# DeltaNet and gated FFN on one core: inverting the first two pairs' blocks in their own layout, and another order of work

## The chip, the cores and the metric

The kernel runs on one core of a Trainium2 chip. The metric is the device time of one execution in microseconds (us), lower is better. The engines are TensorE (PE; its weight loads are listed as PEld), VectorE (DVE), ScalarE (ACT), GpSimd (POOL) and SyncE (SP). SP only issues DMAs; ACT issues some too, and POOL a few at the start.

## The reference, cut to what matters

```python
B, H, S, D = 4, 8, 768, 48
def attn(q, k, v, beta):
    k_n = k / (norm(k, axis=-1) + 1e-6)
    state = zeros((B, H, D, D))
    for t in range(S):
        y[:, :, t] = einsum('bhd,bhde->bhe', q[:, :, t], state)
        v_old = einsum('bhde,bhd->bhe', state, k_n[:, :, t])
        state += beta[:, :, t] * outer(k_n[:, :, t], v[:, :, t] - v_old)
x = y.transpose(0, 2, 1, 3).reshape(B * S, H * D)      # 3072 x 384
h = x @ w_in                                           # w_in 384 x 2048
out = (h * cos(h)) @ w_out                             # w_out 2048 x 384
```

All of it is float32. The inputs w_in and w_out arrive in a 64-bit format, which the kernel takes apart into words.

## The kernel before

**Units and pairs.** The sequence is cut into 24 units of 32 tokens (`NU`, `C`). Within a unit the recurrence becomes a triangular system for each of the 32 (batch, head) blocks. For unit n the kernel turns keys and queries (`turn`), multiplies them with the keys (`gram`, tile p_g), scales the key part into a triangular block g (`gram_keys`) and masks the query part into tt (`gram_queries`). Then it applies the state to keys and queries (`through_state`, p_kq), subtracts (`right_side`), solves with the inverse of the block (`solve`, p_u), updates the state (`update`, p_s), adds the in-chunk part (`within`, p_kq) and turns the result into x (`features`, p_z). Each unit's state needs the unit before it. Two units are a pair m; a pair's 256 tokens are one step p of the feed-forward part.

**Inversion.** Pair m's blocks go to DRAM (`gram_put`, g_dr) and come back with one block on each partition (`gram_get`, gb). `invert` eliminates column by column: a product (line 675, tile part), then a subtraction (line 682, tile z), on POOL. The result goes to DRAM again (`put`, z_dr) and comes back in the layout of the solve (`get`, zt). Pair 0 (`HALVED` = 1) differs: `fold` lays the two 16-wide diagonal blocks of each 32-wide block over each other, the elimination has 15 columns and runs on DVE, and units 0 and 1 are solved in halves: `solve_half` (p_w), `between` with the off-diagonal block (p_v), then `solve` (p_u) from halves_z.

**Feed-forward.** Steps 0 and 1 compute h plainly (`hidden`, p_h, one product for two of the eight groups of 256 columns), later steps with 20 products of sums of x and of w_in (`x_sum` line 968, `in_sums`, `layer` line 1053). Step 0 multiplies with w_out plainly (`output`, line 1076), later ones with seven products (`product` line 1133) of sums of gate blocks (`left_sum`, line 1149) and of w_out (`right_sum`).

**Weights.** 12 tiles of w_in and 16 of w_out are loaded (`narrow_load`, tile pairs of a pool of eight shared with the gates and others), split by ACT (`narrow_split`), shifted by DVE (`narrow_shift`), added by POOL (`narrow_add`).

**Order.** Every step is a task with an engine, dependencies and the buffers it makes and frees. `Order.LINE` is a list of numbers: all tasks in the sequence in which they are written out. Each engine and each DMA queue runs its own in that sequence, and an instruction that waits holds up all behind it on its engine. `Order.OTHER` lists the tasks that go to the other queue (ACT instead of SP) or the other engine (POOL or DVE). Costs and due times in `add` are a planner's; at run time they do nothing.

Of the kernel before, what the change touches and what calls it, by code (L numbers as in the profile page):

```python
# [46 lines left out]
class Order:  # L47

    OTHER = {
        ('gram_put', 0), ('gram_get', 0), ('put', 0), ('q', 3), ('gram_get', 1), ('k', 4),  # L50
        ('gram_get', 2), ('k', 7), ('weights', 3), ('weights', 5), ('weights', 6), ('weights', 9),
        ('weights', 10), ('weights', 14), ('weights', 15), ('weights', 17)
# [3 lines left out]
0 1971 1 2 10 11 12 7 3 37 4 72 14 38 39 42 15 73 1972 13 1975 43 96 1973 97 40 1974 16 44 17 1976  # L56
18 1979 19 45 20 79 46 75 99 76 48 100 77 80 47 1983 78 1980 104 1977 49 81 50 1981 1978 105 1987
82 1982 1984 51 9 101 131 1985 84 52 1991 132 1988 53 36 102 1986 1995 54 155 106 1992 8 55 56 107
108 109 1989 22 1996 1999 1993 1990 134 74 1997 1994 135 1998 110 21 41 111 23 83 2000 138 2003 57
2001 136 139 24 2002 137 2007 156 25 112 26 98 27 28 2004 186 113 29 2011 2008 2005 30 187 32 31  # L60
114 210 2009 140 103 2015 33 58 141 211 142 115 189 143 2012 190 34 2019 59 35 2013 133 2016 60
2006 2017 61 2020 2023 679 116 2021 2018 62 680 684 2027 63 117 681 241 682 2024 683 64 685 2025
2031 689 2022 65 2028 2026 2029 157 118 66 5 6 68 67 2035 69 818 159 265 2032 686 86 687 2033 160
688 2030 690 2039 691 161 2034 2036 119 2010 719 692 2037 2014 162 163 164 693 191 2040 2043 70
822 694 87 71 243 85 165 244 2038 193 695 2041 2047 699 245 194 696 819 697 158 166 88 2042 700
731 704 89 167 2051 2048 698 120 192 2044 90 701 92 168 91 702 709 2045 2055 2052 296 703 93 705
2053 94 714 169 95 706 710 2049 2056 711 707 121 2059 712 708 195 715 2046 747 196 197 198 2050
716 717 170 2063 2060 720 718 122 748 713 749 123 735 2067 2064 2061 752 2054 124 2062 736 171 125
2057 753 2071 127 750 823 320 757 2065 128 126 754 2066 129 751 145 130 2058 755 2075 758 172 214
146 2072 739 762 298 2073 215 299 2068 756 216 248 173 821 721 763 217 2076 2069 2079 764 219 188  # L70
732 767 765 759 766 760 825 2070 772 174 768 2077 247 2080 769 2078 761 770 2074 2081 220 777 771
2082 221 144 740 773 826 300 782 774 269 218 775 778 222 722 829 268 779 776 743 147 723 744 223
780 733 724 725 783 820 212 249 827 302 726 830 224 148 835 303 149 737 213 151 727 152 150 225
175 784 824 351 781 153 176 154 788 785 728 177 226 828 745 270 178 729 179 787 227 831 790 730
789 834 180 793 746 182 375 181 794 183 246 228 184 786 796 185 791 832 250 798 200 792 242 251
799 252 836 253 840 800 741 353 842 839 843 271 801 229 844 851 272 845 738 274 855 841 852 301
846 802 856 273 847 354 324 848 804 803 849 857 734 355 797 859 275 201 853 806 860 199 833 807
854 850 837 742 858 808 266 304 276 866 809 277 323 795 861 867 202 862 870 203 810 278 863 267
864 204 206 357 871 868 207 205 279 874 869 230 231 865 875 356 878 406 805 872 838 811 280 873
232 876 812 879 233 877 898 880 234 813 894 358 882 899 281 235 883 895 237 236 896 430 886 900  # L80
881 208 897 884 209 901 238 814 282 885 325 902 815 887 379 239 816 888 240 903 906 890 953 889
305 904 955 378 907 956 922 306 960 908 905 957 892 307 308 910 958 891 255 954 408 909 959 893
326 297 283 911 925 918 817 919 964 928 912 327 968 923 965 329 929 920 924 969 966 921 972 256
961 967 409 914 962 970 963 284 328 931 971 915 410 330 973 913 979 916 930 981 980 917 974 933
926 983 975 285 927 934 331 984 982 935 332 254 411 985 936 976 987 321 986 937 988 333 359 977
991 412 978 257 992 989 258 1011 939 334 413 990 259 940 261 941 260 993 461 262 1007 932 942 335
994 322 286 943 1008 287 995 944 352 938 336 288 996 945 1009 289 1012 997 290 1013 998 292 376
337 1014 946 291 1015 485 1001 947 1016 263 949 1010 293 264 380 338 999 294 1000 950 295 1002
1017 434 360 1019 951 1005 361 362 1003 1018 948 1020 381 1066 1006 310 1068 1021 1004 1069 339
1031 1035 382 1070 463 384 1071 1032 1077 1067 1022 1081 1072 1078 311 363 1073 1038 1036 1082  # L90
1074 464 1027 1079 1041 309 414 1033 465 1083 1080 383 1042 1037 952 1084 1034 385 1085 386 1076
1028 1087 340 1023 1075 1044 1029 1024 1086 433 312 1094 313 387 1092 1043 468 314 1095 1093 1046
316 1030 1096 317 315 388 1025 467 1098 1088 1097 341 1099 1026 1100 342 435 1047 389 1101 1039
1104 488 1040 1102 1045 343 1103 1048 1105 489 390 1120 1089 1108 344 1090 1106 1049 516 1091 345
347 1109 346 1050 1124 391 1125 1052 1107 1126 318 1054 1112 319 1121 1110 1127 1122 392 1055 1128
540 1123 348 1056 466 1111 349 1057 1114 350 1113 1058 1129 1179 1132 1051 1186 1130 1059 1181
1115 1182 1053 1116 1180 1060 1131 415 1183 1061 1149 365 1184 518 1189 1133 1118 1187 416 1134
417 1185 1062 418 1119 393 1117 436 519 1140 1190 437 1141 1194 439 377 1063 1195 1142 1198 1191
1143 1196 1188 1199 1064 520 1192 1144 1135 394 1148 1193 440 366 438 1197 407 1151 1145 1150 1207
1154 1146 1205 1208 1136 1155 1147 364 1137 1157 1138 1211 441 1159 431 1139 1200 442 1152 1160  # L100
1201 1156 395 1206 1153 367 1209 368 443 1065 1161 1212 1210 369 1162 1158 371 571 370 1213 372
444 1202 1163 469 1203 373 1165 374 1204 1214 396 1167 523 445 1217 490 1215 1218 522 1168 1216
1237 397 1233 1169 1166 446 462 1238 1221 1164 1239 1219 1234 1222 398 1220 1235 1225 399 1223 447
1226 400 1170 1224 1240 402 595 432 1227 1245 403 1171 1236 448 401 1241 1172 1228 1229 1173 1242
544 404 1231 1246 405 1243 1175 1230 1247 1232 1176 573 1248 1292 1293 470 1177 1253 1302 449 420
1244 486 1294 1254 1303 1295 1257 471 1296 1307 1262 1304 1297 473 472 1255 1261 1298 1258 1299
1256 491 1300 1259 1178 419 1264 1301 1308 492 574 1249 1311 421 1174 575 1250 494 1305 1312 487
1267 1309 1306 1320 543 524 1310 1268 1251 1260 1318 493 495 496 1321 1270 1319 1263 578 1252 1313
1265 1322 1314 1324 450 1323 422 1272 1315 497 1273 1266 577 1316 423 1274 1326 1275 498 1325 424
1269 426 626 521 1328 427 1327 425 1276 499 1329 428 1317 451 429 1346 1278 452 1330 1280 500 545  # L110
453 1334 1331 598 454 1281 1350 1335 1271 1282 1347 517 501 1332 1348 1283 1336 1333 599 455 1351
1337 1349 457 1352 1284 1279 458 650 502 1354 1353 1338 456 1340 1277 459 1341 1342 460 1339 1285
1405 1355 541 1407 525 1356 1286 1406 576 1344 1358 1408 1287 526 1409 1288 1359 1410 528 1345 503
1289 1360 527 1361 546 1290 475 1370 1343 628 1416 547 1357 1420 549 629 1366 1374 1411 548 1421
1371 1415 1417 1377 1367 1412 504 1372 1291 630 1418 1375 1380 1376 1422 1419 550 1373 1381 1423
579 1368 1413 1424 1362 1414 1431 1369 474 1425 1363 1426 1432 542 1433 1427 632 1435 551 476 1364
1383 1436 552 1434 505 1439 1428 1437 1365 1440 633 1429 477 1385 553 1438 1443 478 1441 1378 479
1379 481 1442 554 1386 482 1384 1459 1444 1447 1430 1387 480 1448 1463 1460 1445 555 1464 1449
1446 506 1465 1388 1450 1389 507 1461 1466 572 1391 631 556 1467 1462 508 1393 1453 1468 1394 1454
1469 509 1395 557 1470 510 1382 512 511 1457 483 1458 1451 484 600 513 1455 514 1452 530 654 515  # L120
1456 1471 1396 1518 580 1390 1520 1397 1472 596 1521 581 1522 1473 1398 582 1523 1392 1479 583
1525 1529 1399 1519 1474 1533 1530 1524 1480 1400 601 558 1481 1401 602 603 1475 604 1482 1534
1402 634 1531 1403 1535 1532 1476 1483 1487 1526 1536 1484 1528 1490 1477 1404 1527 559 1485 605
1478 1537 1493 1488 1539 1538 1486 1494 1540 1489 1546 1541 1496 1547 1542 560 531 606 1544 1543
# [65 lines left out]
def kernel(  # L190
# [1060 lines left out]
    def unit(n):  # L1251
# [71 lines left out]
        if second:  # L1323
            inverse(m)
# [369 lines left out]
```

## Time and profile before

| | us |
|---|---|
| median of 3 runs | 659.93 |
| lowest, highest | 659.56, 664.02 |
| span of the profiled execution | 657.8 |
| PE busy | 598.3 |
| DVE, ACT, POOL busy | 485.7, 259.7, 448.2 |
| start of the first product of step 0's h | 71.3 |
| end of the last matmul | 652.95 |

The profile is of one execution; its times start at the span's begin. A line of a timeline gives the start, the length, the engine, the line of the kernel, the operation, its tiles (out<-in), shape and count, and in brackets the idle time before it and what ended that. A matmul of float32 leaves two records. Engine rows give busy time; DMA issues and waits are not in it. The chain of waits is followed back from the last instruction, at each step to what released it.

### The profile page before, as it was taken

The numbers are of one execution on the slowest core, as the hardware profiler recorded it, in microseconds if no ns is written. First come the engines' busy times: TensorE is split into PE (matmuls) and PEld (weight loads), VectorE is DVE, ScalarE is ACT, GpSimd is POOL, SyncE is SP. The second block draws the span as 40 slices with busy tenths as digits, with TensorE's granted clock in tenths as the row PEclk, the third lists the DMA queues.
The fourth block names the chain that finished last, engine by engine and source line by source line (L and its number), as shares of the span: only waits on it lengthen the run. The fifth ranks groups of instructions, "written<-read, shape, count | busy, mean of one in ns | idle before, by whom it ended". The sixth has DMA issues, their size and how long they took to land.

```text
span 657.8 us, 27560 instructions
## 1 busy us (share of the span) xinstructions
PE 598.3 (91%) x11960; PEld 561.2 (85%) x11960; DVE 485.7 (74%) x886; ACT 259.7 (39%) x446; POOL 448.2 (68%) x844
## 2 busy tenths in 40 slices
PE   3316889989989999999999999899999999999997
PEld 3305869877889999999999999899999999999996
DVE  6685487878878887877779868778768687566772
ACT  3432456452223542435434523542523534335340
POOL 4458698878888888868968848868688589203000
PEclk9999799989999999999999999999999999999999
DMA  8876674465254453452243454432412400200000
GB/s 171 198 159 150 164 182 124 121 124 75 55 101 70 62 103 61 75 98 45 51 95 53 84 91 67 80 53 37 95 29 43 88 5 15 45 3 26 0 25 25
DMA packets 215644, 51.78 MB, mean 79 GB/s; under 512 B 207076, under 2 KB 210420, under 8 KB 215524
## 3 DMA queue, kind: packets, MB, share of 16 engines
q1 hardware_dynamic: 204516, 43.39, 34.8%
q10 hardware_dynamic: 10752, 6.20, 3.7%
q8 instruction: 94, 1.54, 1.0%
q0 software_dynamic: 256, 0.44, 0.3%
q14 instruction: 26, 0.21, 0.1%
HBM read 39.24 MB, written 10.75 MB: 76 GB/s over the span
## 4 chain that ended last, share of the span: by engine, by line
PE 52%; POOL 23%; DMA 10%; SPq 5%; issue 5%; DVE 4%; ACT 1%; ACTq 0%; POOLq 0%; DVEq 0%
PE p_out L1133 19%; PE p_h L1053 19%; POOL part L675 10%; POOL z L682 10%; PE p_h L875 3%; DMA qp<-in_q_dram 3%; PE p_kq L732 2%; DMA gb<-g_dr 2%; PE p_u L795 2%; PE p_s L818 2%; PE p_kq L835 2%; PE p_o L1133 2%; DMA g_dr<-g 1%; DMA pairs<-in_moe_w_in_dram 1%; POOL x_sum L968 1%
## 5 line engine op out<-in xcount | busy, mean ns | idle before, releaser
L675 POOL TENSOR_TENSOR part<-z,gb 128x126 f32<-128x126 f32 (+22 forms) x341 | 154.0, 452 | 57.2 <-DMA gb<-g_dr 15.4
L682 POOL TENSOR_TENSOR z<-z,part 128x126 f32<-128x126 f32 (+22 forms) x341 | 155.4, 456 | 26.7
L1133 PE MATMUL p_out<-w_out,g_ffn 128*128 128x192 f32 x672 | 121.2, 328 | 0.4 <-ACT o L1172 0.4
L1133 PEld LDWEIGHTS p_out<-w_out,g_ffn 128*128 128x128 f32 x672 | 107.8, 190 | 1.7 <-ACT o L1172 0.6
L1133 PE MATMUL p_out<-w_sum,g_ffn 128*128 128x192 f32 x496 | 89.1, 329 | 0.3 <-issue 0.3
L932 ACT ACTIVATE turns<-turns,halfpi 128x512 f32<-128x512 f32 x96 | 68.3, 720 | 47.0 <-DVE turns L923 46.8
L1053 PE MATMUL p_h<-x_sum,w_in 128*128 128x128 f32 x640 | 83.2, 278 | 1.7 <-POOL x_sum L968 1.7
L1133 PEld LDWEIGHTS p_out<-w_sum,g_ffn 128*128 128x128 f32 x496 | 79.7, 190 | 1.2 <-issue 0.4
L1053 PEld LDWEIGHTS p_h<-x_sum,w_in 128*128 128x128 f32 x640 | 77.3, 192 | 3.5 <-POOL x_sum L968 2.1
L1149 DVE TENSOR_TENSOR g_ffn<-g_ffn 128x512 f32<-128x512 f32 x88 | 64.5, 737 | 12.6 <-PE p_out L1133 11.7
L916 ACT ACTIVATE turns<-g_ffn,quarter_turn 128x512 int32<-128x512 f32 x70 | 50.4, 720 | 55.9 <-DVE g_ffn L1070 37.2
L1070 DVE TENSOR_TENSOR g_ffn<-g_ffn,p_h 128x512 f32<-128x512 f32 x80 | 54.0, 682 | 15.8 <-PE p_h L1053 13.1
L935 DVE TENSOR_TENSOR g_ffn<-turns,g_ffn 128x512 f32<-128x512 f32 x70 | 52.9, 758 | 11.3 <-ACT turns L932 11.3
L923 DVE SCALAR_TENSOR_TENSOR turns<-g_ffn,turns 128x512 f32<-128x512 f32 x70 | 52.8, 760 | 8.4 <-ACT turns L916 8.2
L1053 PE MATMUL p_h<-x_sum,in_sum 128*128 128x128 f32 x400 | 53.4, 278 | 2.0 <-POOL x_sum L968 1.5
L875 PE MATMUL p_h<-x_ffn,w_in 128*128 128x128 f32 x384 | 49.5, 289 | 2.9 <-DVE g_ffn L935 2.3
L1053 PEld LDWEIGHTS p_h<-x_sum,in_sum 128*128 128x128 f32 x400 | 49.4, 192 | 3.0 <-POOL x_sum L968 1.7
L875 PEld LDWEIGHTS p_h<-x_ffn,w_in 128*128 128x128 f32 x384 | 47.3, 203 | 4.2 <-issue 2.4
L1185 DVE SCALAR_TENSOR_TENSOR o<-p_out,o 128x192 f32<-128x192 f32 x74 | 25.2, 353 | 31.8 <-PE p_out L1133 30.8
L486 POOL TENSOR_TENSOR knrm<-ksum,halves 128x16 f32<-128x16 f32 (+1 forms) x14 | 38.5, 2752 | 11.1 <-DVE ksum L474 10.9
L1053 PE MATMUL p_h<-x_ffn,w_in 128*128 128x128 f32 x320 | 42.5, 277 | 0.0
L1053 PEld LDWEIGHTS p_h<-x_ffn,w_in 128*128 128x128 f32 x320 | 39.2, 192 | 0.4
(122 smaller groups left out, 933.2 us busy)
## 6 DMA issues: line engine op xcount, KB each, us to landing
pairs<-in_moe_w_out_dram SPq DMA_DIRECT2D x13, 384.0 KB
vp<-in_v_dram SPq DMA_DIRECT2D x96, 48.0 KB
gb<-g_dr SPq DMA_DIRECT2D x18, 256.0 KB
out_dram<-o SPq DMA_DIRECT2D x23, 192.0 KB
pairs<-in_moe_w_in_dram SPq DMA_DIRECT2D x7, 512.0 KB
kp<-in_k_dram SPq DMA_DIRECT2D x128, 24.0 KB
z_dr<-z SPq DMA_DIRECT2D x11, 256.0 KB
zt<-z_dr SPq DMA_DIRECT2D x88, 32.0 KB
```

The source lines that it names most:

```text
L486: nc.gpsimd.tensor_tensor(out=scales[m][2][:, part], in0=sums[m, part.start][:, 0:n], in1=halves[:, 0:n], op=ALU.pow,)
L675: eng.tensor_tensor(out=part, in0=z[:, 0:rows, j, None].to_broadcast(shape), in1=a[:, j, None, j + 1 :].to_broadcast(shape), op=ALU.mult,)
L682: eng.tensor_tensor(out=behind, in0=behind, in1=part, op=ALU.subtract)
L875: nc.tensor.matmul(p_h[:, i], w_in[:, t, (4 * k + i) * 128 : (4 * k + i + 1) * 128], xts[p][:, t, unit * 128 : (unit + 1) * 128], start=(i ...
L916: nc.scalar.activation(turns[p, f], hidden_of(p, f), AF.Identity, bias=quarter_turn, scale=TURN)
L923: nc.vector.scalar_tensor_tensor(out=r, in0=hidden_of(p, f), scalar=TURN, in1=t, op0=ALU.mult, op1=ALU.subtract,)
L932: nc.scalar.activation(r, r, AF.Sin, bias=halfpi, scale=2.0 * math.pi)
L935: nc.vector.tensor_tensor(out=place(p, f), in0=step_of(rests.pop((p, f)), f), in1=step_of(hidden_of(p, f), f), op=ALU.mult,)
L1053: nc.tensor.matmul(p_h[:, e], in_block(*w)[:, e], x_of(p, b), start=new and e == 0, stop=True, skip_group_check=True,)
L1070: nc.vector.tensor_tensor(out=part_of(p, to), in0=part_of(p, one), in1=part_of(p, two), op=op)
L1133: nc.tensor.matmul(p_o, left(p, part, a)[:, e % 4], right(e, b), start=(e == 0), stop=(e == FT // 2 - 1), skip_group_check=True,)
L1149: either(("left", p, x, s), nc.vector, nc.gpsimd).tensor_tensor(out=left(p, s, to), in0=left(p, s, one), in1=left(p, s, two), op=op)
```

## The change

- Pairs 0 and 1 (`ROWED` = 2) are both inverted as 16-blocks, in the layout in which their products come: rows of a block on partitions. Matmuls with 0/1 matrices (`picks`, made on DVE in memory that w_sum uses later) copy row j of each 16-block to all 16 of its partitions in PSUM (`rows`, p_r). Units 0 and 1 are eliminated on DVE, each by itself (groups 0 and 1); units 2 and 3 together on POOL (group 2), for which ACT copies the rows from PSUM (`rows_copy`).
- The DRAM passages of pairs 0 and 1 and pair 1's inversion of 31 columns are gone. Units 2 and 3 are now solved in halves too. ACT takes part in `fold` and `unfold`.
- Weights are staged in six slots in in_sum and w_sum; a load waits for the addition of the tile six places before it.
- The table load of ACT's sine comes first on ACT; the far part of the constants is loaded later, by SP; beta is spread in two parts; `scale` and `weigh` are split into smaller tasks.
- The dependency of each plain hidden product on the one before it is gone, and a hidden step's g tile is made at the gate.
- `LINE` and `OTHER` are new: 36 load, store and transfer tasks go to ACT's queue instead of 7, 61 sums of x go to DVE, 37 sums of gates to POOL, and a few sums of weights change engine.

```diff
-    HALVED, HC = 1, C // 2
+    ROWED, HC = 2, C // 2
...
+    halfpi = const.tile([128, 1], FP, name="halfpi")
+    nc.gpsimd.memset(halfpi, math.pi / 2.0)
+    warm = const.tile([128, 1], FP, name="warm")
+    nc.scalar.activation(warm, halfpi, AF.Sin)
+
     load(0, "k")
     load(0, "q", nc.scalar)
...
+    picks = w_sum[:, 0 : FT // 4].rearrange("p e a c -> p (e a c)")[
+        :, 0 : (HC - 1) * 128
+    ].rearrange("p (j m) -> p j m", m=128)
+
+    def make_picks(js):
+        by_row = ident.rearrange("p (g r) -> p r g", r=HC)
+        nc.vector.tensor_copy(
+            picks[:, js].rearrange("p j (g r) -> p j g r", r=HC),
+            by_row[:, js, :, None].to_broadcast([128, js.stop - js.start, 128 // HC, HC]),
+        )
...
+    stages = [
+        in_sum[:, 2 * i : 2 * i + 2].rearrange("p a e c -> p (a e c)") for i in range(4)
+    ] + [
+        w_sum[:, FT // 4 :].rearrange("p e a c -> p (e a c)")[:, i : i + 4 * TOK]
+        for i in (0, 4 * TOK)
+    ]
...
-        pairs = ffn_pool.tile([128, 4, TOK], U32, name="pairs", tag="g", bufs=GATES)
-        words[t] = pairs.rearrange("p a t -> p (a t)")[:, 0 : 2 * n]
+        words[t] = stages[t % len(stages)].bitcast(U32)[:, 0 : 2 * n]
...
+    GROUPS = [(0,), (1,), (2, 3)]
+    ON_POOL = (2,)
...
+    def rows(r, s):
+        f, x = of_group(r)[0], of_group(r)[3]
+        p_r = p_rows[r, s] = bank("h", [128, 4 * H * HC], "p_r").rearrange(
+            "p (j x i) -> p j x i", x=x, i=HC
+        )
+        js = rows_at(r, s)
+        for k, j in enumerate(js):
+            i = 1 + (js[0] if r in ON_POOL else j)
+            nc.tensor.matmul(
+                p_r[:, k, :, i:], picks[:, j], f[:, :, i:],
+                start=True, stop=True, skip_group_check=True,
+            )
...
+    def eliminate(r, s):
+        f, z, scratch, x = of_group(r)
+        eng = nc.gpsimd if r in ON_POOL else nc.vector
+        p_r = p_rows.pop((r, s))
+        for k, j in enumerate(rows_at(r, s)):
+            part = scratch[:, :, j + 1 :]
+            eng.tensor_tensor(
+                out=part,
+                in0=z[:, :, j, None].to_broadcast([128, x, HC - 1 - j]),
+                in1=p_r[:, k, :, j + 1 :],
+                op=ALU.mult,
+            )
+            behind = z[:, :, j + 1 :]
+            eng.tensor_tensor(out=behind, in0=behind, in1=part, op=ALU.subtract)
+
+    def unfold(n):
+        zts[n] = half_zt[n]
+        z = row_tile(n)[:, 0, n % 2, :, HC:]
+        for a in range(2):
+            to = zts[n][:, :, HC * a : HC * a + HC]
+            if ("unfold", n) in Order.OTHER:
+                nc.scalar.activation(to, z, AF.Copy, scale=in_half[:, a : a + 1])
+            else:
+                nc.vector.tensor_scalar(to, z, in_half[:, a : a + 1], None, op0=ALU.mult)
...
-        if n < 2 * HALVED:
+        if n < 2 * ROWED:
             add(("solve_half", n), "PE", few, lambda: solve_half(n), ready,
...
         add(("weights", t), "SP", 0.45, lambda: narrow_load(t),
-            [("weights", t - 1)] if t else [],
-            makes=[("g", ("pairs", t))], moves=1.8 * c, due=LOADS + 2 * t)
+            ([("weights", t - 1)] if t else [])
+            + ([("add", t - len(stages))] if t >= len(stages) else []), moves=1.8 * c, due=LOADS + 2 * t)
```

## The prediction

> **What bounds the kernel now.** I read the page's engine shares, then busy time by stage, then PE's timeline at the start, the chain of waits, and the rows that price the new work.
>
> ```profile
> span 657.8 us, 27560 instructions
> ...
> PE 598.3 (91%) x11960; PEld 561.2 (85%) x11960; DVE 485.7 (74%) x886; ACT 259.7 (39%) x446; POOL 448.2 (68%) x844
> ```
>
> By stage: its ends and length (us), busy us of PE, PEld, DVE, ACT and POOL with their counts, then clock, DMA share, GB/s.
>
> ```profile
> 0.00:71.30 71.30, 27.68 (x844) 23.03 (x844) 46.66 (x125) 25.50 (x46) 43.01 (x64) 0.95 0.72 166
> 71.30:101.00 29.70, 26.62 (x568) 23.94 (x567) 20.53 (x34) 16.98 (x32) 23.75 (x33) 0.94 0.77 189
> 101.00:154.50 53.50, 51.07 (x1004) 45.68 (x1004) 42.18 (x75) 26.90 (x49) 44.44 (x85) 0.97 0.51 109
> 154.50:470.90 316.40, 310.94 (x6693) 292.21 (x6693) 251.78 (x440) 122.22 (x207) 258.59 (x506) 1.00 0.42 71
> ```
>
> PE idles 71.3 - 27.7 = 43.6 us before 71.3 and only 59.5 - 43.6 = 16 afterwards. Its work is the bound once it has work, so a gain must come from the start. PE's timeline there:
>
> ```profile
> 49.84 1.81 PE L762 MATMUL p_w<-vp,halves_z 32*32 32x48 f32 x64 [1.16 <-ACT kq_t L544]
> ...
> 69.47 1.90 PE L762 MATMUL p_w<-rhs,halves_z 32*32 32x48 f32 x64 [2.20 <-ACT x_ffn L862]
> 71.29 4.50 PE L875 MATMUL p_h<-x_ffn,w_in 128*128 128x128 f32 x24
> 75.73 0.88 PE L762 MATMUL p_v<-u_half,halves_z 32*32 32x48 f32 x64
> 76.54 2.94 PE L875 MATMUL p_h<-x_ffn,w_in 128*128 128x128 f32 x24
> ...
> 101.16 1.10 PE L795 MATMUL p_u<-rhs,zt 32*32 32x48 f32 x60 [0.34 <-DMA zt<-z_dr]
> ```
>
> Unit 0's first solve (p_w) waits until 49.8 because pair 0's blocks go through DRAM before and after the inversion; unit 2's (p_u, 101.2) because pair 1's inversion holds POOL from 50.3 to 89.4. The passages, in the chain of waits:
>
> ```profile
> 19.19 5.80 DMA g_dr<-g
> 25.55 3.25 DMA gb<-g_dr
> ...
> 50.40 5.16 DMA halves_z<-z_dr
> ...
> 90.51 4.01 DMA z_dr<-z
> ...
> 96.13 4.98 DMA zt<-z_dr
> ```
>
> One elimination step (a product, then a subtraction) on DVE and on POOL, from their timelines:
>
> ```profile
> 33.16 0.23 DVE L675 TENSOR_TENSOR part_v<-p_i,gb 128x64 f32<-128x64 f32 x1
> 33.42 0.23 DVE L682 TENSOR_TENSOR p_i<-p_i,part_v 128x64 f32<-128x64 f32 x1
> ```
>
> ```profile
> 63.10 0.43 POOL L675 TENSOR_TENSOR part<-z,gb 128x136 f32<-128x136 f32 x1
> 63.61 1.22 POOL L682 TENSOR_TENSOR z<-z,part 128x136 f32<-128x136 f32 x1
> ```
>
> **PE's ledger.** I price every matmul of both orders by late, undisturbed rows: 8 records of p_h 0.89, 8 of p_out 1.30 (2.69 when 384 wide), a state product 1.30, a Gram, p_w, p_v, p_u or in-chunk product 0.81, p_s 0.82, p_z 0.33, a turn 1.04. Before: 569.8 us. After adds p_w and p_v of units 2 and 3, 4 x 0.81 = 3.2, and 45 row-copying matmuls, 3952 columns at 1.30/8/192 = 0.85 ns, at least 0.03 us each, 3.5: 576.5.
>
> **The start, queue by queue.**
> - ACT's table load and warm-up (1.28 + 0.20) now precede q's DMA issues: q lands 1.5 later and unit 0's Gram ends at 11.7. Weights 0, issued behind q at 8.4, land after 4.1 to 5.4 (chain rows at 7.19 and 13.72). On ACT their split (1.25) and a square (0.5) stand ahead of the first fold, so folding ends at 16.5.
> - Group 0: 30 DVE operations of 64 elements on average, 0.26 apart as above, 7.8. Held up until unit 1's Gram at 20.9, it ends at 27.5. Gone are 8.7 us of old elimination (28.9 to 37.6) and three DRAM passages.
> - Unfolding (0.7) and a seam bring unit 0's p_w to 28.4. The old trace takes 11.0 from there to p_kq (49.84 to 60.85); weight shifts of 1.02 share DVE: 38.7. Then a turn 2.1, p_z 0.9, ACT's copy 0.5, state 1.8, a Gram 1.2, all at the slow prices of the old start: first p_h at 44.7, not 71.3.
> - DVE from 38.3: group 1 7.8, two scales 1.4, a shift 1.0, a sum 0.95, three Gram readings 1.3, folds 0.7, unfolding 0.6, waits 0.7: unit 1's blocks at 52.8, its chain over near 65, between hidden products.
> - Group 2's rows reach POOL, copied by ACT, at 55.9. POOL's operations start 0.32 apart at 31 elements and 0.51 at 136, hence 0.50 at its mean of 128: 30 take 15.0. By mean rows (0.366 at 31, 0.51 at 126, plus 0.08 between) 17.7. With five weight additions of 1.39 it ends at 78 to 81; I take 80, since DVE is full beside it.
> - Unfolding, p_w, a copy, p_v and a subtraction queued behind four DVE operations: unit 2's p_u at 84, not 101.2.
>
> The Trainium skill ("SBUF — State Buffer", Who interferes with whom) says that a VectorE instruction with two SBUF inputs and a GpSimd instruction reading SBUF exclude each other. It speaks against a change that eliminates on both, and the trace agrees in kind (the subtraction of 1.22 above; its mean is 0.61). By the rule group 2 costs 17.7 or more, by undisturbed rows 15.0.
>
> Weights do not hold this up: eighteen loads of 0.197 MB, twelve of 0.524 and the constants are 10.1 MB, 61 us at 166 GB/s, but w_in's last addition stands behind group 2 and a norm on POOL (near 86) anyway, and only hidden products after unit 2's p_u need it. Staging costs nothing while additions free the six slots in time; a late one holds SP's later k, q and v loads with it, 4.1 to 5.4 a tile. Picks and the split of beta and scales (3 us on DVE) lie beside loading before 10 us, or cost 3.
>
> **Sum.** At unit 2's p_u, before has 39.6 of its ledger behind it, after 43.7. From there before loses (652.95 - 101.16) - (569.8 - 39.6) = 21.6 over the ledger. Of this 4.9 falls before unit 4's p_u (154.49), mostly one wait for a gate near 142 and the slow matmuls behind it; I keep half: 19.1. The end comes 4.9 after the last matmul, as now. After: 84 + (576.5 - 43.7) + 19.1 + 4.9 = 640.8; the profiled execution lies 2.1 under the runs' median: 643.
>
> **Moved work later.** ACT issues 36 tasks of loads, stores and transfers instead of 7, and its activations queue behind those that wait; it is 39% busy, and SP's queue shrinks. POOL hands 61 sums of x (0.62) to DVE (0.2 to 0.42 each, from 128x256 at 0.41) and takes 37 gate sums: DVE loses 27 and gains 12 to 26; POOL loses 38 and gains 51 (1.39, as the weight additions of that size; bounds 1.28 and 1.66). In stage 154.5:470.9 DVE has 65 us free and POOL 58: costed at nothing. If that cover is gone, the first rival prices it.
>
> **Rivals.**
> - *POOL paces the middle.* From pair 2's inversion (102.9) to the end of pair 9's (470.9) the old trace takes 368.0. The new order adds there 14 gate sums and 3 input sums (1.39), 10 weight operations (1.06), less 48 x sums: +4.5. Begun at 88.5, with the old waits (24 us, most for DMA), pair 9 ends at 461; its p_u follows 11.3 later, as now. Only 394.6 of the ledger is done there: 472.3 + 181.9 + 2.9 of loss + 4.9 + 2.1 = 664, slower than before by 4. The forecast has that p_u at 84 + 350.9 + 16.2 = 451, so this decides once the inversion ends after 440. For it: POOL and DMA fill the old chain from 280 to 420. Against: there PE still idles only 5.5 of 316 us.
> - *PE stays slow.* p_h took 4.50 at 71.3, then 2.94. The new start is sparse; if the four hidden products just before unit 2's p_u run slow, 4 x 1.56 = 6.2: 649. Against: they stand close together. The Trainium skill ("TensorE: Matmul & The Clock Gate", The HAM clock gate) gives half rate until about 3.4 us of sustained work, and again after as long an idle window; the first p_h agrees.
> - *The start moves less.* DVE or ACT queues run 12 late: 655.
> - *Later stalls vanish too.* Half of PE's 16 us: 635.
>
> That the change does less than it says is excluded: the new order holds no transfer of pairs 0 and 1.
>
> **Numbers.** A measurement of this kernel can tell about 1% from no change (653.3 to 666.5). Forecast 0.58 (637 to 650), POOL 0.14, slow PE 0.08, late start 0.08, fewer stalls 0.12. Faster: 0.58 + 0.08 + 0.12 = 0.78. The POOL case spreads upward, 0.08 within 1% and 0.06 slower; with the late start, same is 0.16. The range 633 to 658 holds forecast, slow PE, late start and half of the fewer-stalls case, 0.80, and group 2's bounds.
>
> **What would show it.** First p_h near 45, unit 2's p_u near 84; group 2 at 15 to 18 us of POOL without its additions; from 150 on no waits of PE for zt. I am wrong if PE waits for zt or for sums in the middle, if p_h starts after 55, or if PE idles over 25 us after it.

## The result and the profile after

The changed kernel takes 700.86 us (median of 4 runs, 695.4 to 703.94) and the kernel before 661.88 on the same chip: ratio 1.058, 95% interval 1.051 to 1.064. It is slower by 39 us; the forecast was 643. The page's head, span and engine shares:

```profile
span 693.6 us, 28213 instructions
...
PE 630.0 (91%) x12306; PEld 587.5 (85%) x12306; DVE 495.9 (72%) x942; ACT 263.8 (38%) x463; POOL 454.5 (66%) x800
```

The profiled execution is one of the quicker ones, so differences between profiles understate those between medians by some 5 us here. TensorE is still the engine that is busy throughout, with 31.7 us more of busy time, of which my ledger prices only 6.7 (the row copies p_r alone keep it busy for 18.8 us at the start, where the ledger has 3.5). By stage, with the same ends and columns as in the prediction, and the last stretch added:

```profile
0.00:71.30 71.30, 53.83 (x1351) 48.19 (x1352) 57.11 (x158) 34.56 (x70) 37.90 (x47) 0.93 0.66 155
71.30:101.00 29.70, 24.77 (x507) 23.38 (x506) 21.98 (x41) 14.87 (x30) 20.41 (x32) 0.89 0.62 149
101.00:154.50 53.50, 51.68 (x996) 41.86 (x995) 45.12 (x77) 25.49 (x48) 47.97 (x69) 1.00 0.47 104
154.50:470.90 316.40, 291.20 (x6236) 273.30 (x6225) 233.18 (x423) 110.33 (x187) 238.93 (x469) 0.98 0.41 68
470.90:693.60 222.70, 208.56 (x3240) 200.78 (x3238) 138.56 (x247) 78.59 (x131) 109.30 (x187) 0.97 0.17 33
```

The last stretch of the kernel before:

```profile
470.90:657.80 186.90, 181.99 (x2858) 176.31 (x2856) 124.59 (x214) 68.11 (x114) 78.40 (x161) 1.00 0.15 31
```

By stage, the first row is the gain: PE is busy twice as long before 71.3 us. The fourth and the fifth are the loss: PE idles 25.2 and 14.1 us there, where it idled 5.5 and 4.9, and its clock is 0.98 and 0.97 instead of 1.00. The start, in PE's timeline:

```profile
28.43 0.88 PE L866 MATMUL p_w<-vp,halves_z 32*32 32x48 f32 x64 [1.40 <-issue]
...
44.63 2.05 PE L979 MATMUL p_h<-x_ffn,w_in 128*128 128x128 f32 x16
...
80.22 0.88 PE L866 MATMUL p_w<-rhs,halves_z 32*32 32x48 f32 x64 [0.59 <-DVE halves_z L746]
...
86.59 4.64 PE L979 MATMUL p_h<-x_ffn,w_in 128*128 128x128 f32 x21 [3.48 <-issue]
91.16 1.01 PE L899 MATMUL p_u<-u_half,halves_z 32*32 32x48 f32 x64
```

And what PE waited for from 72 us on (engine, line, releaser; total us, times, longest):

```profile
PE p_kq L836 <- issue: 8.5, 7, 2.0
PE p_u L899 <- DMA zt<-z_dr: 8.0, 3, 6.2
PE p_g L627 <- issue: 3.6, 2, 2.9
PE p_h L979 <- issue: 3.5, 1, 3.5
PE p_h L1157 <- ACT p_h L1169: 3.1, 1, 3.1
```

In the kernel before, the longest wait on "issue" and the one on zt are:

```profile
PE p_kq L732 <- issue: 2.9, 2, 1.9
PE p_u L795 <- DMA zt<-z_dr: 0.3, 1, 0.3
```

Two things stand out. "Issue", time in which PE waited for nothing that the profile shows, comes to 19.8 us over all lines; in the kernel before it is 3.7. And zt, on which PE waited 0.3 us, now costs 8.0.

To see where the time goes I set each unit's p_u against the ledger. From unit 2's p_u to the last matmul the kernel before takes 21.6 us over its priced work, the changed one (687.8 - 91.2) - (576.5 - 43.7) = 63.8. PE is idle for 8.1 of the 21.6 and for 35.3 of the 63.8; the other 15 us of the difference are slower matmuls. The granted clock is part of that: it was half for 24 us of this stretch (258.7 to 265.6, 289.5 to 292.9, 436.2 to 439.6, 504.5 to 507.9 and 542.0 to 548.9), and in the kernel before for 3.4 us (142.9 to 146.3). This makes some 10 of the 15.

### The profile page after: what moved, and what is told of

Same layout as the page of the kernel before. It is cut to its first block, busy times and chain, and to the rows that moved or that the text cites. A ratio compares the mean times of both kernels' runs of the same rounds, so it can differ in the third digit from the quotient of the medians.

```text
span 693.6 us, 28213 instructions
## 1 busy us (share of the span) xinstructions
PE 630.0 (91%) x12306; PEld 587.5 (85%) x12306; DVE 495.9 (72%) x942; ACT 263.8 (38%) x463; POOL 454.5 (66%) x800
## 4 chain that ended last, share of the span: by engine, by line
PE 68%; POOL 8%; DVE 7%; issue 5%; DMA 5%; SPq 3%; ACT 2%; ACTq 0%; POOLq 0%; DVEq 0%
PE p_out L1237 24%; PE p_h L1157 23%; PE p_h L979 4%; PE p_kq L836 3%; PE p_u L899 3%; POOL part L799 3%; PE p_s L922 2%; POOL z L806 2%; PE p_kq L939 2%; PE p_r L709 2%; PE p_g L627 2%; SPq L360 2%; DMA zt<-z_dr 1%; PE p_o L1237 1%; DVE turns L1027 1%
## 5 line engine op out<-in xcount | busy, mean ns | idle before, releaser
L799 POOL TENSOR_TENSOR part<-z,gb 128x126 f32<-128x126 f32 (+22 forms) x310 | 137.2, 443 | 42.8 <-DMA gb<-g_dr 17.0
L806 POOL TENSOR_TENSOR z<-z,part 128x126 f32<-128x126 f32 (+22 forms) x310 | 141.5, 457 | 24.3
L1237 PE MATMUL p_out<-w_out,g_ffn 128*128 128x192 f32 x672 | 124.9, 334 | 2.8 <-DVE o L1289 1.6
L1237 PEld LDWEIGHTS p_out<-w_out,g_ffn 128*128 128x128 f32 x672 | 110.0, 193 | 5.2 <-DVE g_ffn L1039 1.7
L1253 POOL TENSOR_TENSOR g_ffn<-g_ffn 128x512 f32<-128x512 f32 x37 | 50.2, 1365 | 68.2 <-PE p_out L1237 33.6
L1157 PE MATMUL p_h<-x_sum,w_in 128*128 128x128 f32 x640 | 89.2, 288 | 4.1 <-ACT p_h L1169 3.1
L1157 PEld LDWEIGHTS p_h<-x_sum,w_in 128*128 128x128 f32 x640 | 82.4, 201 | 6.1 <-issue 4.4
L1174 DVE TENSOR_TENSOR g_ffn<-g_ffn,p_h 128x512 f32<-128x512 f32 x80 | 54.3, 680 | 20.6 <-PE p_h L1157 19.6
L979 PEld LDWEIGHTS p_h<-x_ffn,w_in 128*128 128x128 f32 x384 | 46.2, 199 | 5.2 <-issue 4.2
L543 POOL TENSOR_TENSOR knrm<-ksum,halves 128x16 f32<-128x16 f32 (+1 forms) x14 | 36.8, 2626 | 16.9 <-DVE ksum L531 16.9
L836 PE MATMUL p_kq<-st,kq_t 48*32 48x48 f32 x2944 | 34.6, 215 | 9.8 <-issue 9.8
```

Source lines behind the costliest of these rows:

```text
L799: nc.gpsimd.tensor_tensor(out=part, in0=z[:, 0:rows, j, None].to_broadcast(shape), in1=a[:, j, None, j + 1 :].to_broadcast(shape), op=ALU. ...
L806: nc.gpsimd.tensor_tensor(out=behind, in0=behind, in1=part, op=ALU.subtract)
L836: nc.tensor.matmul(p_kq[quarter(b), par, a, j], kq_t[rows48(par), a, b * NP + j], st[rows48(par), b // 2, j, b % 2], start=(j == 0 and a = ...
L979: nc.tensor.matmul(p_h[:, i], w_in[:, t, (4 * k + i) * 128 : (4 * k + i + 1) * 128], xts[p][:, t, unit * 128 : (unit + 1) * 128], start=(i ...
L1157: nc.tensor.matmul(p_h[:, e], in_block(*w)[:, e], x_of(p, b), start=new and e == 0, stop=True, skip_group_check=True,)
L1174: nc.vector.tensor_tensor(out=part_of(p, to), in0=part_of(p, one), in1=part_of(p, two), op=op)
```

## Experiments

Times are medians; a ratio is to the kernel before on the same chip, with its 95% interval. "Fillers" are matmuls of 8x8 that nothing reads.

### Which half loses

The first run joins the new start to the old rest, the second the old start to the new rest. LINE and OTHER are cut at a task; a task that would come before its dependencies is put off until they are done. The lists are long, so here is the first edit in words:

```diff
-    LINE = the changed kernel's tasks in its order
+    LINE = those up to ("solve", 4), then the others in the order of the kernel before
-    OTHER = the changed kernel's
+    OTHER = the changed kernel's up to ("solve", 4), for the others those of the kernel before
```

> The changed kernel up to unit 4's solve; every later task in the order of the kernel before, on the engine and the DMA queue it had there. At unit 4's p_u the changed kernel stood at 153.4 us with 102.7 us of priced TensorE work done, 473.8 to go. THEORY ORDER (the rest of the rewritten order loses, the start gains): the old rest lost 16.7 us beyond its work from there, so the last matmul is at 153.4 + 473.8 + 16.7 = 644 and the run at about 651 us. RIVAL START (the new start leaves something behind, late buffers or a slow clock, that costs whatever follows): still 690 to 700 us.

700.84 us, ratio 1.057 (1.049 to 1.065).

> The kernel before, with its old inversion, up to unit 8's solve; every later task in the changed kernel's order, on its engines and queues. The kernel before stood at 245.7 us there with 174.1 us of its TensorE work done. The changed kernel lost 43.2 us beyond its work from unit 8 to its last matmul. THEORY ORDER: 245.7 + 395.7 + 43.2 + 6.6 behind the last matmul = 691 us. RIVAL START: the rest loses what it lost before, so 660 us.

689.32 us, 1.039 (1.033 to 1.045). So neither of the two accounts holds alone: both joins lose. In the first, 20.6 us are one wait of my own making (PE for u behind ACT, which stood 12.4 us for keys loaded late), but 18.2 us are "issue" stalls, nearly 15 of them after unit 4's solve, where its order is that of the kernel before, which has 3.7 in all.

The next two leave the order and move tasks back: the first run the 37 gate sums, the 61 x sums and the 38 DMA tasks of ACT's queue, the second the DMA tasks alone. (With three loads of weights, which stay, the change puts 41 tasks on that queue, and the kernel before has 16, eight of them loads of weights; the 36 and 7 of the description and the prediction are counted wrong.) A few of the tasks taken out:

```diff
     OTHER = {
-        ('left', 1, 4, 0), ('x_sum', 2, 'd'),
...
-        ('store', 1, 0), ('blocks', 10, 0), ('v', 7),
...
```

> The changed kernel with the same order, but 61 x sums and 37 left sums on the engines they had before, and 38 DMA tasks (stores, blocks, v, gram and inverse transfers) back on SP's queue. If the assignment alone makes the loss: about 645 to 655 us. If the order alone makes it: 695 to 705 us. If both share it: 665 to 685 us.

773.74 us, 1.166 (1.160 to 1.172). The new order needs its sums where they are; POOL cannot deliver them at their new places:

```profile
PE p_h L1140 <- POOL x_sum L1055: 64.4, 14, 13.9
```

> The changed kernel with the 38 DMA tasks back on SP's queue, the sums left where the change puts them. THEORY QUEUE (activations wait behind DMA issues on their queue, and transfers arrive late): 660 to 675 us, and the 6.2 us wait of p_u for zt at 261 us is gone. RIVAL SUMS (37 left sums on POOL, 61 x sums on VectorE): no change, about 700 us, and the old-assignment run takes it all. THEORY ORDER: about 700 us in both.

680.08 us, 1.027 (1.021 to 1.032), against 1.058: the queue is worth 20 us. "Issue" stays at 18.4.

### Where the instructions stand in their blocks

The queue table of the changed kernel has this row (packets, MB, share):

```profile
q8 instruction: 97, 1.59, 0.9%
```

That is 16.4 KB a packet. The trace has 12306 matmuls, 12306 weight loads and 172 further instructions of PE, most of them waits: 255.5 to a packet. In the kernel before it is 24069 instructions and 94 packets, 256.1. The packets are PE's program, fetched 256 instructions at a time. A state product p_kq has 128 records of each, one whole packet, and runs in 1.3 us; 24 records of p_h, 48 instructions, take 2.9. Here is one of the stalls in the changed kernel:

```profile
285.10 0.80 PE L627 MATMUL p_g<-kq_t 48*32 48x64 f32 x60
...
285.74 1.03 PE L836 MATMUL p_kq<-st,kq_t 48*32 48x48 f32 x90
288.79 0.57 PE L836 MATMUL p_kq<-st,kq_t 48*32 48x48 f32 x37 [2.02 <-issue]
289.30 1.97 PE L1157 MATMUL p_h<-x_sum,w_in 128*128 128x128 f32 x8
```

PE stops in the middle of a product whose operands have long been there, after 90 records. The 128 records before the stop, 256 instructions, ran in 1.46 us; with the stall of 2.02 the next packet came 3.5 us after the last. Five such stops in Gram and state product together (after 232, 288 and 420 us here, at 289 and 418 in the run without DMA on ACT's queue) give 3.3 to 3.8. They are block ends: counted over all instructions of PE in the order of their starts, the stops of over 0.5 us in the latter run stand at places 3265, 6594, 7105, 8129, 9153, 10946, 11969, 12738, 14785, 16065 and 16833, and each leaves 193 or 194 when divided by 256. The same holds for 102 of the 103 issue stalls of over 0.5 us after 72 us in the profiles of all twenty kernels, and each of the 102 ends 1.2 to 1.7 us after a packet of q8 has landed. So what PE waits for there is its program.

Two things bring such a stall about. Either PE uses a block up before the next can have come: before the stops at 232, 288 and 420 us the packet starts 0.9 to 1.0 us after the first instruction of the block, takes 0.9 to 1.2, and PE goes on 1.4 to 1.5 later. Or, on top of that, the packet comes late: before the stalls at 86.6, 171.6 and 435.0 us, the three longest, it starts 3.5, 3.7 and 2.1 us after it. Why it is late there is not shown.

In the list above, the last row is the second half of the price: the eight records of p_h after the stall take 1.97 us, not 0.99, and the granted clock from 289 to 292 us is 0.58.

So I walked both orders: every record at its warm duration, a cut every 256 instructions at that remainder, and 3.4 us less the block's duration lost at each block that is shorter (an estimate from these stops, which knows nothing of late packets). The kernel before comes to 5.1 us, the changed one to 25.0. What differs is where the cuts fall. The change puts some 690 loads and matmuls more ahead of the rest, so the same order of the rest is cut elsewhere, which would be why the first join stalls. Fillers move the cuts and nothing else:

```diff
+    filler = const.tile([128, 8], FP, name="filler")
+    nc.gpsimd.memset(filler, 0.0)
     load(0, "k")
...
+    for _ in range(28):
+        nc.tensor.matmul(p_out[0:8, 0, 0:8], filler, filler, start=True, stop=True)
     lasts, done = {}, [len(nc.cur_bb.bb.instructions)]
```

> The kernel before, unchanged but for 28 filler matmuls of 8x8 in front of its first transpose, while TensorE waits for its first input: 112 more TensorE instructions (each fp32 matmul is two weight loads and two matmuls), so every later instruction stands 112 places further in the blocks of 256 in which the instruction queue's 97 packets of 16 KB bring them. THEORY FETCH: TensorE stalls where a block of 256 is used up in under about 3.4 us, the time of a refill worked out from the stalls; walking the order with the warm durations gives 5 us of stalls at this kernel's own place, and 27 us with 28 fillers. So 22 us of issue stalls more, and the slower clock behind each of some ten stalls: 685 to 700 us. RIVAL (order or queues make the loss, where the blocks begin is nothing): 660 us, within 3 us.

> Control: 64 such fillers, 256 instructions, one whole block, so that every later instruction stands at the same place in its block as in the kernel before. THEORY FETCH: 660 to 665 us, the time of the kernel before with at most the fillers' own few us. If fillers as such cost time (a late start, another clock): as much as with 28 or more.

> The changed kernel with 20 fillers, 80 instructions. THEORY FETCH: the walk gives 25 us of stalls at the changed kernel's own place and 9 us with 20 fillers, so 16 us less, and some 8 us less of slow clock: 672 to 682 us; what is left over the kernel before is the DMA on ACT's queue (20 us in the run without it). RIVAL: 700 us.

> The kernel before with 12 fillers. The walk gives 14.4 us of stalls, against 5.1 with none and 26.6 with 28, where 21.5 us more of it became 21 us more of time: 660 + 9 + 1 for the fillers = 668 to 673 us. If only some places hurt and not the sum of the short blocks: 660 to 664 or over 680 us.

| kernel | walk, us | "issue" after 72 us | time | ratio |
|---|---|---|---|---|
| before | 5.1 | 3.7 | 660 | 1 |
| before + 12 | 14.4 | 10.0 | 665.85 | 1.009 (1.005 to 1.012) |
| before + 28 | 26.6 | 21.3 | 682.24 | 1.035 (1.029 to 1.041) |
| before + 64 | 5.1 | 2.8 | 664.79 | 1.006 (1.002 to 1.009) |
| changed | 25.0 | 19.8 | 700.86 | 1.058 (1.051 to 1.064) |
| changed + 20 | 9.2 | 7.7 | 685.93 | 1.038 (1.033 to 1.044) |

Twenty-eight idle matmuls make the old kernel 3.5% slower, 64 make it 0.6% slower. What stalls in the former, by the waits of PE:

```profile
PE p_g L567 <- issue: 8.5, 4, 2.9
PE p_kq L734 <- issue: 7.1, 7, 1.9
```

The walk is too high each time (by a fifth to four fifths of what was measured), keeps the order of the six, and missed the sizes at both ends: with 28 fillers and with 20 the time came out under and over the range (682 against 685 to 700, 686 against 672 to 682), and with 12 also under it (666 against 668 to 673).

The Trainium skill ("Runtime: NRT & Kernel Launch", Instruction fetch mechanics) says that the engine fetches the next block of 256 while it runs the current one, and that the cost of a block's end is mostly hidden. The blocks agree with the trace. Mostly hidden it is behind p_h and p_out; behind Gram and state product side by side it is up to 2.9 us a time here.

### The stores on ACT's queue

> The changed kernel with the 38 DMA tasks back on SP's queue and 20 fillers. If the two causes add (20.8 us for the queue, measured without fillers, 14.9 for the blocks, measured with the queue): 700.9 - 20.8 - 14.9 = 665 us. If they are one loss seen twice (a late transfer and a stall behind it): 678 us or more.

669.65 us, 1.011 (1.004 to 1.018): the two causes add, 1.9 points for the blocks and 3.1 for the queue alone, 4.7 together. The next run sends back the stores alone (the first three of the 15):

```diff
     OTHER = {
-        ('store', 0, 0), ('store', 0, 1), ('store', 1, 0),
...
```

> The changed kernel with 20 fillers and only the 15 stores of the output back on SP's queue; the other 23 DMA tasks stay on ACT's. THEORY LANES: transfers of both queues share eight completion semaphores in the order of the program, so SP's next load on a store's semaphore waits until ACT has reached, issued and landed the store (SP stood still from about 255 to 259.7 us until a store landed, and zt came 6 us late). Then the stores make most of the 20 us: 668 to 674 us, and the longest wait of p_u for zt is under 2 us. RIVAL (ACT's activations stand behind the loads that it issues): 682 to 688 us, and the waits of PE for ACT stay at 8 us.

667.54 us, 1.011 (1.004 to 1.018), a little under the range. These are all 15 stores, and they are the whole of it; the other 23 tasks may stay on ACT's queue. In the changed kernel, SP's and ACT's timelines, SP's waits over the whole run, and PE's timeline show how:

```profile
251.47 11.50 SPq L819 DMA_DIRECT2D zt<-z_dr  x8
```

```profile
255.06 0.58 ACTq L1301 DMA_DIRECT2D out_dram<-o  x1
```

```profile
SPq L819 <- DMA out_dram<-o: 9.5, 3, 7.7
```

```profile
261.54 1.81 PE L899 MATMUL p_u<-rhs,zt 32*32 32x48 f32 x62 [6.21 <-DMA zt<-z_dr]
```

In the trace the transfers of both queues take eight completion semaphores in turn (signals that a transfer has landed), and an issue waits for the last user of its semaphore. A store stands in ACT's queue until ACT has come to it and its sum is there. SP has issued one of its eight loads of zt at 251.5 and stops for 7.7 us before the second, whose semaphore the store has: the store is issued at 255.06 and lands at 259.68, SP goes on at 259.70, and PE stands behind. With the stores on SP's queue that wait is 1.3 us at most, and PE's for zt are:

```profile
PE p_u L1005 <- DMA zt<-z_dr: 2.4, 3, 1.0
```

These waits are the smaller part of the 18 us (23 between the two profiles). From the run with 20 fillers to this one PE's idle time after unit 2's p_u falls from 31.5 to 20.1 us: for zt from 8.3 to 2.4, for ACT from 8.1 to 4.0, "issue" from 7.6 to 4.1. The time over the ledger in which PE is not idle falls by as much, from 30 to 19 us; the granted clock was half for 24 us between 100 and 660 us there and is not reduced between 85.4 and 660 us here. So the rival has a share too, the waits for ACT, but they do not stay at 8 us.

The same move alone in the kernel before:

> The kernel before with its 15 stores issued from ACT's queue, nothing else changed. THEORY LANES: 15 to 20 us slower, 670 to 680 us, as the changed kernel gained 18 us when its stores went back, with SP's loads standing still behind stores that ACT has not reached. If the stores hurt only in the changed order: 660 to 664 us.

666.15 us, 1.008 (1.004 to 1.011): 5 us, not 15 to 20. SP then stands 38.5 us behind stores with its k and v loads, and PE hardly notices: its idle time after 72 us is 15.5 us instead of 11.

### Can the start's lead be kept?

With both causes mended the kernel is 24 us over the forecast. Five joins with the old rest try to keep the lead: with 20 fillers and the cut at unit 3's solve; at 4 with the late task of the first join moved; at 6; at 4 again with keys 10 and 11 and v 7 loaded earlier; at 11 with 24 fillers.

> The changed kernel up to unit 3's solve, then the order, engines and queues of the kernel before, with 20 fillers. THEORY FETCH: the new start's gain of 11 us at that solve is kept less the 9.6 us of it that is only work not yet done, 6 us of stalls stand where the walk gives 19 without fillers: 645 to 660 us. THEORY START (the new start leaves something behind that costs whatever follows): 680 us or more, as in the run of the same kind without fillers.

664.80 us, 1.006 (1.003 to 1.009).

> The changed kernel up to unit 4's solve, but all its DMA tasks of that part on SP's queue; then the order, engines and queues of the kernel before, with the 13 tasks that the old order has before that solve left at their new place (pair 5's norms among them: in the first run of this kind ACT stood 12.4 us for their keys and TensorE 20.6 us behind that); 20 fillers. THEORY (start gains, blocks and queue lose): at unit 4's p_u 102.7 us of work done at 153.4 us, 473.8 to go, the old rest's loss of 16.7 and 2.5 us more of stalls: last matmul at 646 us, run 650 to 656 us. RIVAL (the lead of the start is given back whatever follows, because gates and weights are not ready): 660 to 667 us, as the one with the cut at unit 3.

671.46 us, 1.017 (1.010 to 1.024).

> The same with the cut at unit 6's solve. At that p_u the changed kernel with 20 fillers stood at 201.5 us with 143.4 us done, 433.1 to go; the old rest's loss from there was 13.8 us, and the walk gives 5 us more of stalls: last matmul at 653 us, run about 660 us. If the old order fits the changed buffers badly at any cut: 670 us or more.

681.64 us, 1.031 (1.024 to 1.038).

> The changed kernel up to unit 4's solve, its stores on SP's queue, keys 10 and 11 loaded ahead of the first store and v 7 behind v 6 (in the run before, DVE stood 13.4 us for v 7 behind 16 loads of keys, and TensorE 15.4 us behind that); then the old order, engines and queues; 20 fillers. With the stores back unit 4's p_u came at 148.7 us with 102.7 us of work done. THEORY (the start's lead can be kept): 148.7 + 473.8 + 16.7 + 3 of stalls = 642 us for the last matmul, 647 to 655 us in all. RIVAL (the lead is always given back): 660 us or more.

666.31 us, 1.010 (1.007 to 1.013).

> The same with the cut at unit 11's solve, 24 fillers (the walk's best place for this order). With the stores back and 20 fillers its p_u came at 301.1 us with 240.4 us done, 336.1 to go; the old rest lost 8.7 us from there, 3 us more of stalls: last matmul at 649 us, run 652 to 658 us. If the lead goes whatever the order: 665 us, as with the changed order kept to the end.

674.06 us, 1.019 (1.015 to 1.024).

All five miss, by 5 to 22 us, the time that keeping the lead would give, and none beats the kernel before. Each join still has waits of its own at the seam (15.4 us for st behind a late v in the second, 10.4 for tt and 6.2 for gates in the third, 4.2 for DVE's sums of weights and 3.3 for x sums in the fourth), so they show that the lead was not kept, not that it can't be. The fourth says most: behind the seam, from unit 8 on, it loses 13 us as the kernel before does (11.5), and it ends 6 us later (666.31 against 660.22), about as much as its added matmuls are priced at (6.7).

The last two runs take work from POOL, my first rival's bound:

```diff
             behind = z[:, 0:rows, j + 1 :]
-            nc.gpsimd.tensor_tensor(out=behind, in0=behind, in1=part, op=ALU.subtract)
```

> The changed kernel with its stores on SP's queue and 20 fillers, without the subtractions of GpSimd's inversions (310 instructions, some 145 us of its busy time, so that the inverse is the unit matrix): half of the work of the chain that gives the units their zt. THEORY POOL (the inversions set the pace of the units from 150 us on: pair 3's starts at 150.3 us, in the kernel before at 150.6, although TensorE is 14 us ahead): a good part of the 36 us lost after unit 4's solve goes, 635 to 650 us. RIVAL (the waits for o, y, gates and zt's own transfer keep the time): 658 us or more, within 1% of the same kernel with the subtractions.

668.02 us, 1.013 (1.010 to 1.016), against 667.54 with the subtractions: no gain. POOL does not pace the changed order: unit 18's p_u, the first of pair 9, comes at 471.6 us, and with the subtractions at 468.8. The profile hides a smaller effect. PE's waits after unit 2's p_u, "issue" left out, fall from 16.0 to 10.2 us, but "issue" grows from 4.1 to 8.9 with the same places of the blocks (some of its packets start late), and the granted clock is half for 6.8 us more. So some 6 us may still be POOL's; the 17 us or more of THEORY POOL are excluded.

> The kernel before without the same subtractions for pairs 2 to 11 (305 instructions). THEORY POOL: it loses only 16.6 us after unit 4's solve, so at most some 10 us go: 650 to 657 us. RIVAL: 658 to 661 us.

650.84 us, 0.987 (0.985 to 0.990). The kernel before does gain, 8.6 us, and its PE is idle for 1.8 us after unit 2's p_u instead of 8.1. The rest goes with the clock at least in part: 0.999 over the span instead of 0.990.

## Why the prediction was wrong

**The bound and the start: right.** Unit 0's p_w came at 28.43 (28.4), the first p_h at 44.63 (44.7). Group 2 kept POOL busy for 7.2 + 8.3 = 15.5 us, and took 17.4 with the gaps, as the forecast counted them (15.0 to 17.7); it ended at 78.6 (78 to 81), and unit 2's p_w stood at 80.2. One price was wrong and did no harm: the 45 row copies leave 90 records, so at 0.85 ns a column and record they cost 6.7 us, not 3.5. All of them come before unit 2's p_u, so the sum from there on does not change.

**Unit 2's p_u at 84: 7 us off.** It came at 91.2: 3.5 of "issue" in the p_h ahead of it, and 21 records in 4.64 us instead of 2.6. That is the rival of slow p_h, with a stall that it did not have. With 20 fillers it came at 87.7.

**The step that failed is in the sum: "I keep half: 19.1".** I took the loss after unit 2's p_u from the old order and let it hold for a new one; it was 63.8. With it fell "costed at nothing" for the moved work. The runs put in its place, between 643 and 700.9 (the medians, from different chips, give 15, 18 and 24.5 us):
- 1.9 points of the ratio, 13 us, for where PE's instructions stand in their blocks (shown by fillers in both directions). My ledger counted added matmuls by duration; that they move all later ones in the blocks was in no step.
- 2.7 points, 18 us, for 15 stores on ACT's queue (shown). I named what queues behind a waiting DMA on ACT and priced it at nothing; PE's waits for ACT lose 4 us of it. That SP's loads stand behind stores, through the shared semaphores, was in no step; it costs 6 us of waits for zt. The rest is 3.5 us of "issue" and matmuls at a reduced clock.
- 24 us that stay with both mended (667.5): unit 2's p_u 2.8 later than forecast, a loss after it of (658.4 - 86.8) - 532.8 = 38.8 instead of 19.1, and 2 us of end and median. That kernel has 17 waits of PE of at most 1.9 us there, 16.0 us in all, for o, y, gates, x sums and zt, 4.1 us of "issue", and 18.7 us over the ledger in which PE is not idle (13.5 in the kernel before), at a clock that is not reduced. Which edit of the order makes them is open.

**The rivals.** "POOL paces the middle" has nearly the right value (664) for the kernel with 20 fillers and its stores back, even the end of pair 9's inversion (461), but the wrong cause, so this is luck: without half of the inversions' work it stays at 668. Its condition, that inversion ending after 440, was met in the changed kernel (479), as in the kernel before (471), and decided nothing. "Fewer stalls" is out: they became more. The signs I gave for being wrong, PE waiting for zt and over 25 us of idling, both came.

**The range** left out a cost that the moved transfers and the new sequence could have, because I asked only whether another engine had free time, not whether the new sequence meets it.

## What to carry to other kernels

Count instructions, not only time: where an engine runs 256 small instructions in some 1.5 us, such groups should not stand side by side, and an edit far ahead of them can cost or save some per cent by moving the block ends; a few dozen idle matmuls test it (12 made the kernel before 0.9% slower, 28 3.5%). Where queues share completion semaphores, a transfer that waits long, here a store, holds up the other queue, so it belongs where its wait is short; what that costs depends on the order (18 us here, 5 us in the kernel before). A loss measured on one order is not a property of the kernel: reprice it when the order is rewritten.

## What was not expected of the hardware

- PE stalls at the ends of its 256-instruction blocks: by 0.6 to 2.9 us at the eight stops of over 0.5 us in Gram and state product of the changed kernel, with 3.3 to 3.8 us from one block to the next at the five looked at above. The stall ends 1.2 to 1.7 us after the packet has landed, whatever the work; so it goes by the block's duration and by when the packet starts.
- After a stall of only 2.02 us the clock was 0.58 from 289 to 292 us. The 27 us of added idle time came with 15 us of slower matmuls. The Trainium skill ("TensorE: Matmul & The Clock Gate", The HAM clock gate) has the clock halve after an idle window of about 3.4 us; here a shorter stop, with small products ahead of it, was enough.
- The kernel before, bound by PE with 8.1 us of idle time left after unit 2's p_u, still gained 8.6 us when half of POOL's inversion was left out, 6.3 of them idle time.
